# Attention and two mixture-of-experts layers on one core: the attention stage's order planned with other lengths, hops and due times

## The chip, the cores and the metric

The kernel runs on one core of one Trainium2 chip, as one program. The metric is device time in microseconds, the median of the runs shown. A core has five instruction queues that run side by side: TensorE (PE; its weight loads are listed apart as PEld), VectorE (DVE), ScalarE (ACT), GpSimd (POOL) and SyncE (SP, which here only issues DMA transfers). Each queue starts its instructions strictly in the order in which the program holds them.

## The reference

The output is a chain of three layers in float32.

- Attention over 2 batches, 8 heads, 768 tokens, head width 64. Each query and key gets a 6-bit bucket from the signs of a projection; a query sees only the keys of its own bucket: `scores = where(q_bucket == k_bucket, q·k/8, -1e9)`, softmax over keys, times `v`.
- A first mixture of 8 experts (512 to 1024 to 512) over the 1536 token rows. The router is `argmax` of the normalised row against normalised expert vectors; `out[mask] = gate * (relu(x[mask] @ w1[e]) @ w2[e])`, one expert for a token.
- A second mixture of 8 experts of the same shape with noisy logits; each token takes its best two experts and sums them by softmax weights.

## The kernel before

A float32 product is made of two or three matmuls on operands that are split into a high and a low part, so beside TensorE's work ACT makes high parts and DVE or POOL makes low parts.

**The attention stage.** The 16 (batch, head) pairs are `h`, and each has two halves of 384 queries, `g = 2h` and `g = 2h+1`, so there are 32 groups. For each group the program does, on the engines named:

- three score steps `sc` (PE, `score_pe`, line 606, four matmuls each), each into one of two PSUM buffers `S`; `mx` (DVE, line 611) takes the row maximum, `ms` (POOL, lines 616 and 617) turns it into a scale and a bias, `ex` (ACT, line 621) writes the exponentials `es` and so frees the `S` buffer;
- six transposes `tr` (PE, line 629, three matmuls each) into one of three PSUM buffers `ET`; `th` (ACT, line 633) and `tl` (DVE, line 639) split the result into `eh` and `el` and free the buffer;
- three steps `pv` (PE, lines 657 and 658, four matmuls), then `fa` (ACT), `fp` (PE, line 667, into an `ET` buffer) and `fo` (DVE, lines 681 and 683), which write the normalised rows to `xrow`.

Once per head there are also the loads of `qk` and `vr`, the split `ph` (ACT) and `pl` (POOL), the copies `hc` and `lc` (six DMAs on SP, lines 520 and 560), the bucket signs: `bp` (PE, line 579, two steps of three matmuls, each into an `ET` buffer), `bt` (DVE, line 588, two steps), and `bs`, a small DMA `ka<-qa` (SP, line 593). The first score of a head waits for that DMA.

**Other work in the same stage.** SP also writes zero rows into `xs` and `out` (line 466, 52 transfers), loads the first weights of the experts (`wraw`, line 204) and writes the rows to `xd` (line 784). ACT and POOL split four weight pieces (lines 213 and 219). When the eight groups of one half batch are done, their three row tiles are routed. Tiles `T0 = 0` can be routed after group 14, `T0 = 3` after group 15, `T0 = 6` and `T0 = 9` after groups 30 and 31. One routing is: squares of rows `rsa`, `rsb` (ACT, line 693); `r7` (DVE, line 705); `rm` (DVE, lines 699, 290, 292, 294); `rr0`, `rr` (PE, lines 243 to 253); `rq` (DVE, lines 299 and 301); `rp` (DVE, lines 266 and 269); `rn` (POOL, lines 306 to 308); `rv` (DVE, lines 311 and 312); `re` (ACT, line 315); `rg` (DVE, lines 319 to 321); three scatters `ra` (POOL, line 729, indirect DMAs of 128 rows); `rc` and `ro` (POOL). Then `e0l` (SP, line 741) loads expert 0's rows `x<-xs`; its four products with the identity and `xo` (PE, lines 745 and 780) come at the end of the stage.

**What sets the order.** Each step is given to a planner (`Plan`) with an engine, a length, a due time, the steps it depends on and the buffers it takes. The planner walks through time. On each engine it looks at the first 60 steps by due time, works out when each could start (after its dependencies, plus a hop between engines from the table `HOP`, plus a latency for DMAs), and among those that could start within `WAIT` of the first it takes the one with the least due time. What comes out is only the order of each engine's queue; on the chip each step then waits for what it needs. The two expert layers are a second `Plan` with its own steps; they begin with the matmuls of line 1062.

Of the kernel before, what the change touches and what calls it, by code (L numbers as in the profile page):

```python
# [18 lines left out]
NB, NHEAD, S, DH = 2, 8, 768, 64  # L19
# [13 lines left out]
CB = float(2.0 ** 30)  # L33
TINY = 1.1754943508222875e-38

HOP = {("PE", "ACT"): 200, ("PE", "DVE"): 200, ("ACT", "PE"): 285, ("DVE", "PE"): 280, ("POOL", "PE"): 210,
       ("ACT", "DVE"): 155, ("DVE", "ACT"): 155, ("DVE", "POOL"): 160, ("ACT", "POOL"): 120,
       ("POOL", "ACT"): 80, ("POOL", "DVE"): 90}
WAIT = 120
PR = dict(sc=-5.4, mx=-8.7, ex=-5.34, pv=3.37, fin=3.38, bits=-14.64, prep=-18.57, load=-37.69, h=-17.66, l=0)  # L40
OFF = ()
WA, WB, WS0 = 8, 5, 8
# [5 lines left out]
FSE, PVN, HLN, ESN = 0, 2, 5, 7  # L48
# [9 lines left out]
class Plan:  # L58

    def __init__(self, rings):
        self.rings = rings
        self.steps = {}

    def add(self, name, eng, dur, fn, due, deps=(), use=(), new=(), lat=0):
        self.steps[name] = (eng, dur, fn, due, tuple(deps), tuple(use) + tuple(new), tuple(new), lat)

    def order(self):
        users = {}  # L70
        for n, st in self.steps.items():
            for k in st[5]:
                users[k] = users.get(k, 0) + 1
        left, free_at, held = dict(users), {}, {r: [] for r in self.rings}
        fin, queue, clock = {}, {}, {}
        for n, st in sorted(self.steps.items(), key=lambda z: z[1][3]):
            queue.setdefault(st[0], []).append(n)
            clock[st[0]] = 0.0
        out = []
        total = sum(len(q) for q in queue.values())  # L80
        while len(out) < total:
            best = None
            for eng, q in queue.items():
                cand = []
                for n in q[:60]:
                    _, dur, _, due, deps, use, new, lat = self.steps[n]
                    t = clock[eng]
                    ok = True
                    for d in deps:
                        if d not in fin:  # L90
                            ok = False
                            break
                        t = max(t, fin[d][1] + (0 if fin[d][0] == eng else fin[d][2] + HOP.get((fin[d][0], eng), 150)))
                    if not ok:
                        continue
                    for r, k in new:
                        h = held[r]
                        if len(h) >= self.rings[r]:
                            o = (r, h[len(h) - self.rings[r]])
                            if left[o]:  # L100
                                ok = False
                                break
                            t = max(t, free_at[o] + (280 if eng == "PE" else 150))
                    if ok:
                        cand.append((t, due, n))
                if cand:
                    t0 = min(c[0] for c in cand) + WAIT
                    c = min((c for c in cand if c[0] <= t0), key=lambda z: z[1])
                    if best is None or c[0] < best[0]:
                        best = (c[0], eng, c[2])  # L110
            if best is None:
                raise RuntimeError("plan stuck: " + str({e: q[:3] for e, q in queue.items()}))
            t, eng, n = best
            _, dur, fn, due, deps, use, new, lat = self.steps[n]
            queue[eng].remove(n)
            for r, k in new:
                held[r].append(k)
            clock[eng] = t + dur
            fin[n] = (eng, t + dur, lat)
            for k in use:  # L120
                left[k] -= 1
                free_at[k] = max(free_at.get(k, 0), t + dur + lat)
            out.append((t, len(out), n))
            self.starts = out
        self.span = max(clock.values())
        return [self.steps[n][2] for _, _, n in sorted(out)]
# [7 lines left out]
def lsh_attention_moe_moe2_kernel(  # L134
# [310 lines left out]
    en = rt.tile([E, D], F32, name="en", bufs=1)  # L445
# [178 lines left out]
    EH, EL, ET, OA, OS, FO = {}, {}, {}, {}, {}, {}  # L624
# [158 lines left out]
    def r1_keep(T0):  # L783
# [1 line left out]
                          xrow[:, T0:T0 + 3, :D])  # L785


    plan = Plan(dict(S=2, ET=3, O=1, es=ESN, eh=HLN, el=HLN, ec=2, os=2, qk=3, vr=3, hx=2, lx=2, qb=2, vh=3,
                     qa=2, sm=3, rt=2))
    add = plan.add  # L790
    P = lambda f, *a, **k: (lambda: f(*a, **k))
# [5 lines left out]
    for h in range(HEADS):  # L797
        z = 12 * h
        due = lambda k, o=0.0: z + PR[k] + o
# [52 lines left out]
    for g in range(NG):  # L852
        h = g // 2
        z = 6.0 * g
        for j in range(3):
            k, o = (g, j), 2 * j
# [50 lines left out]
    for c in range(8):  # L907
        add(("wr", c), "SP", 1700, P(wload, c), (WR if c < WP else 150) + c, ([("in", 2)] if c < WP else [("in", 18 + CAP1 // 16)]) + ([("wl", c - 4, 7)] if c > 3 else []),
            lat=2500)
# [5 lines left out]
    for i, g in enumerate((14, 15, 30, 31)):  # L915
        T0, z = 3 * i, 6.0 * g + 8.5 + (L1 if i < 2 else 0)
        zg = z if i < 2 else z + 8 if i == 2 else z + 4
        hot = [("fo", x) for x in range(g % 2 + 16 * (g // 16), g + 1, 2)]
        w = L2 if i < 2 else .1
# [25 lines left out]
                [("rm", T0), ("rr0", T0)] + prev, **U)  # L945
        add(("ro", T0), "POOL", 1064, P(r1_over, T0), z + 9, [("rp", T0), ("ra", 9 if i > 1 else T0, 2)], **U)
        add(("rk", T0), "SP", 1500, P(r1_keep, T0), z + (3 if i < 3 else 0), hot)
    add(("e0l",), "SP", 2000, x0_load, 160, [("ra", 3, 2)], lat=2500)
    for d in range(4):
        x0 = [(("S", "x0"), ("ET", "x0"))[d // 2]]  # L950
        add(("e0t", d), "PE", 430, P(x0_tr, d), (180, 180, 195.1, 195.2)[d], [("e0l",), (("tr", 31, 1), ("pv", 30, 5), ("pv", 31, 5), ("pv", 31, 5))[d]] + ([("e0t", d - 1)] if d else []),
# [1 line left out]
    for i, T0 in enumerate((6, 9)):  # L953
        z = 6.0 * (30 + i) + 8.5
# [350 lines left out]
    add = plan.add  # L1305
# [24 lines left out]
    for key in range(2 * E):  # L1330
# [64 lines left out]
        t = z + 16 * q  # L1395
# [224 lines left out]
```

## Time and profile before

| | us |
|---|---|
| median of 3 runs | 784.34 |
| the runs | 784.03, 784.34, 788.62 |
| the profiled execution, its own time | 788.22 |
| its span from first to last instruction | 786.5 |

The profiled execution is near the slowest of the three runs, 3.88 above the median. In the span PE is busy 97%, PEld 94%, DVE 72%, ACT 60% and POOL 49% of the time. TensorE's granted clock is 0.995 of full speed on average. The attention stage takes the first 277.7 us: the first matmul of line 1062 starts there. A busy share over the whole span mixes the three layers; the tables by stretch and the lists in order of time are what to read. Times in such rows are in us from the start of the span; a start is exact to 0.01, the end of a matmul is modelled, so gaps are read from start to start.

### The profile page before, as it was taken

The page shows a single profiled execution, that of the slowest core. Times are in us where ns is not written, and L with a number is a line of the kernel's source. Part 1 is how long each engine was busy: PE and PEld are TensorE (multiplying, and loading weights), DVE is VectorE, ACT ScalarE, POOL GpSimd, SP SyncE. Part 2 cuts the span into 40 slices and gives each one's busy share as a digit, 9 for nine tenths or more (in the row PEclk, how much of TensorE's full clock was granted, in tenths as well). Part 3 has the DMA queues.
Part 4 walks back from the last instruction along what each step waited for, and adds up shares of the span by engine and source line. Part 5 has one row for each costly group of instructions (what it writes and reads, how often), then busy time and mean ns, then how long its engine had stood idle before and what let it go on. Part 6 is the DMA issues. An engine that isn't in the chain of part 4 may idle for free.

```text
span 786.5 us, 15056 instructions
## 1 busy us (share of the span) xinstructions
PE 759.5 (97%) x5094; PEld 735.8 (94%) x5094; DVE 565.9 (72%) x1265; ACT 473.2 (60%) x1009; POOL 384.8 (49%) x679
## 2 busy tenths in 40 slices
PE   8999999898999999999999999999999999999996
PEld 6999999787999889999999998999999999999995
DVE  8999999986989868878867767684575566565511
ACT  7899999776888747656656555454344435354310
POOL 7555654773442360443224334028374564748384
PEclk9999999999999999999999999999999999999998
DMA  7697778897662257976678656867796675866333
GB/s 188 160 281 219 173 197 239 233 243 235 148 162 58 80 163 237 274 241 192 206 237 238 214 173 187 181 182 152 168 229 146 165 175 126 178 155 108 93 34 83
DMA packets 92964, 140.64 MB, mean 179 GB/s; under 512 B 25898, under 2 KB 56898, under 8 KB 92882
## 3 DMA queue, kind: packets, MB, share of 16 engines
q1 hardware_dynamic: 75618, 122.93, 55.5%
q0 software_dynamic: 17264, 16.69, 11.7%
q8 instruction: 42, 0.69, 0.4%
q14 instruction: 40, 0.33, 0.1%
HBM read 88.54 MB, written 34.46 MB: 156 GB/s over the span
## 4 chain that ended last, share of the span: by engine, by line
PE 81%; DVE 7%; ACT 4%; DMA 3%; issue 2%; POOL 2%; POOLq 0%; another core or an unknown queue 0%; SPq 0%; ACTq 0%; DVEq 0%
PE ET L1086 9%; PE ET L1088 9%; PE S L1062 9%; PE ET L1087 9%; PE S L1064 9%; PE S L1063 9%; PE S L606 7%; PE ET L629 6%; PE O L657 3%; PE O L658 3%; PE ET L667 2%; PE ET L579 2%; DMA wraw<-in_w2a_dram 2%; PE ET L1131 1%; DVE mxs L611 1%
## 5 line engine op out<-in xcount | busy, mean ns | idle before, releaser
L1270 POOL DMA_INDIRECT out_dram<-yo,idx x91 | 148.5, 1632 | 124.6 <-DVE yo L1267 99.0
L1062 PE MATMUL S<-xh,w0h 128*128 128x224 f32 (+1 forms) x512 | 163.3, 319 | 1.4 <-DVE hl L1072 1.0
L1064 PE MATMUL S<-xh,w0l 128*128 128x224 f32 (+1 forms) x512 | 160.6, 314 | 0.0
L1063 PE MATMUL S<-xl,w0h 128*128 128x224 f32 (+1 forms) x512 | 159.5, 312 | 0.3 <-issue 0.3
L1086 PE MATMUL ET<-hh,w1h 128*128 128x224 f32 (+2 forms) x504 | 157.0, 312 | 1.9 <-ACT ys L1110 1.7
L1088 PE MATMUL ET<-hh,w1l 128*128 128x224 f32 (+2 forms) x504 | 156.9, 311 | 0.0
L1087 PE MATMUL ET<-hl,w1h 128*128 128x224 f32 (+2 forms) x504 | 155.8, 309 | 0.0
L1068 ACT ACTIVATE hh<-S 128x448 fp32r<-128x448 f32 (+1 forms) x64 | 45.1, 704 | 126.4 <-PE S L1064 118.7
L1072 DVE SCALAR_TENSOR_TENSOR hl<-S,hh 128x448 fp32r<-128x448 f32 (+1 forms) x64 | 52.4, 819 | 77.8 <-ACT hh L1068 71.7
L621 ACT ACTIVATE es<-S,mxs 128x768 f32<-128x768 f32 x96 | 95.6, 996 | 16.9 <-POOL mxs L617 12.3
L639 DVE TENSOR_TENSOR el<-ET,eh 128x384 fp32r<-128x384 f32 x192 | 99.3, 549 | 8.4 <-ACT eh L633 5.4
L611 DVE TENSOR_REDUCE mxs<-S 128x1 f32<-128x768 f32 x96 | 91.5, 954 | 15.0 <-PE S L606 12.9
L1086 PEld LDWEIGHTS ET<-hh,w1h 128*128 128x128 f32 x504 | 95.6, 190 | 3.7 <-ACT ys L1110 3.5
L1062 PEld LDWEIGHTS S<-xh,w0h 128*128 128x128 f32 x512 | 97.1, 190 | 2.0 <-DVE hl L1072 1.2
L1063 PEld LDWEIGHTS S<-xl,w0h 128*128 128x128 f32 x512 | 97.2, 190 | 1.2 <-issue 0.5
L633 ACT ACTIVATE eh<-ET 128x384 fp32r<-128x384 f32 x192 | 87.1, 492 | 18.3 <-PE ET L629 17.0
L1064 PEld LDWEIGHTS S<-xh,w0l 128*128 128x128 f32 x512 | 97.2, 190 | 0.5 <-issue 0.2
L1087 PEld LDWEIGHTS ET<-hl,w1h 128*128 128x128 f32 x504 | 95.7, 190 | 0.7
L1088 PEld LDWEIGHTS ET<-hh,w1l 128*128 128x128 f32 x504 | 95.6, 190 | 0.2
L219 DVE TENSOR_TENSOR w1l<-wraw,w1h 128x512 fp32r<-128x512 f32 x128 | 81.9, 685 | 15.5 <-ACT w1h L213 13.7
L629 PE MATMUL ET<-idf,es 128*128 128x128 f32 x576 | 85.7, 275 | 0.6 <-DVE enT L503 0.4
L213 ACT ACTIVATE w1h<-wraw 128x512 fp32r<-128x512 f32 x128 | 72.7, 623 | 14.6 <-DMA wraw<-in_w2a_dram 11.6
(260 smaller groups left out, 1443.2 us busy)
## 6 DMA issues: line engine op xcount, KB each, us to landing
wraw<-in_w1a_dram SPq DMA_DIRECT2D x32, 512.0 KB
wraw<-in_w2a_dram SPq DMA_DIRECT2D x32, 512.0 KB
wraw<-in_w1b_dram SPq DMA_DIRECT2D x32, 512.0 KB
wraw<-in_w2b_dram SPq DMA_DIRECT2D x32, 512.0 KB
xs<-zrow SPq DMA_DIRECT2D x26, 260.5 KB
xr<-xs SPq DMA_DIRECT2D x28, 208.0 KB
qk<-in_qk_dram SPq DMA_DIRECT2D x15, 384.0 KB
xs<-zrow SPq DMA_DIRECT2D x14, 261.0 KB
```

Of the source, the lines that this page charges most:

```text
L611: nc.vector.tensor_reduce(MX[(3 * g + j) % 9][:, 0:1], SC[g, j][:, :, :384], axis=AX.XY, op=OP.max, negate=True)
L621: nc.scalar.activation(ES[g, j].rearrange("p (a b) -> p a b", a=2), SC[g, j][:, :, :384], AF.Exp, bias=mx[:, 2:3], scale=mx[:, 1:2], accum ...
L629: nc.tensor.transpose(T[:, j * 128:j * 128 + 128], ES[g, j][:, kb * 128:kb * 128 + 128], idf)
L633: nc.scalar.activation(EH[g, kb], ET[g, kb], AF.Copy)
L639: nc.vector.tensor_tensor(EL[g, kb], ET[g, kb], EH[g, kb], op=OP.subtract)
L1062: nc.tensor.matmul(o, wH[n][:, fs], xh, start=kd == 0, stop=False)
L1063: nc.tensor.matmul(o, wH[n][:, fs], xl, start=False, stop=False)
L1064: nc.tensor.matmul(o, wL[n][:, fs], xh, start=False, stop=kd == 3)
L1086: nc.tensor.matmul(P, wH[n][:, ws], hh, start=f == 0, stop=False)
L1087: nc.tensor.matmul(P, wH[n][:, ws], hl_, start=False, stop=False)
L1088: nc.tensor.matmul(P, wL[n][:, ws], hh, start=False, stop=f == 7)
L1270: s = nc.gpsimd.indirect_dma_start(out=out.rearrange("n (a c) -> (n a) c", a=4), out_offset=bass.IndirectOffsetOnAxis(ap=IDX[e][:, b:b + 1 ...
```

## The change

The change touches the first planner alone, the one of the attention stage; the expert layers keep the default lengths, hops and waits.

- `LENGTH` gives new lengths to about 60 kinds of steps, and to SP's DMAs a new length and latency. `HOP` has new hops; the old table stays as `HOP0`, the default.
- `SHIFT` moves the due times of 34 kinds of steps. The kind is the step's first name, for routing steps with its `T0`, and for `ms` with its engine.
- `WAITS` replaces the one `WAIT` of 120 by a wait of each engine: none on PE, on ACT the larger of 130 and 0.4 of the candidate's length, on DVE 120, on POOL the larger of 120 and the candidate's whole length. A freed PSUM buffer counts as free for PE after 200, before 280.
- `e0l` depends on the last scatter of `T0 = 0` too, not on that of `T0 = 3` alone.

No instruction is added or removed: each of the five queues holds the same instructions as before, in another order, and the order of the expert layers is unchanged on every queue.

```diff
-HOP = {("PE", "ACT"): 200, ("PE", "DVE"): 200, ("ACT", "PE"): 285, ("DVE", "PE"): 280, ("POOL", "PE"): 210,
+HOP = {("PE", "ACT"): 260, ("PE", "DVE"): 280, ("ACT", "DVE"): 149, ("ACT", "POOL"): 195, ("DVE", "POOL"): 169,
...
+LENGTH = {('X4', 'at', 5600): 6800, ('ACT', 'ph0', 412): 407, ('DVE', 'pl0', 469): 466, ('DVE', 'pl', 469): 477, ('DVE', 'sp', 433): 806, ('ACT', 'fk0', 733): 727,
...
+SHIFT = {'bs': 5, 'bt': 15, 'en3': 10, 'fr': -60, 'fs': -40, 'fv1': 40, 'mx': -5, 'oh9': -65, 'ph': -30,
+    'pl': -5, 'pv': 5, 'ra3': 180, 'rc0': 335, 're3': 30, 'rg0': 10, 'rn6': -305, 'ro0': 155, 'rq0': 47,
+    'rq3': 55, 'rr00': 29, 'rsa0': -22.7, 'rsa3': -5, 'rsa6': 15, 'rsa9': 30, 'rsb3': -60, 'rv0': 20, 'rv3': -40,
+    'rv6': -85, 'sc': 3.5, 'th': -4, 'tl': 4, 'tr': 5.3, 'wh': -5, 'xa9': -60}
+WAITS = {'PE': (0, 0.0), 'ACT': (130, 0.4), 'DVE': (120, 0.0), 'POOL': (120, 1.0)}
 WAIT = 120
+ROUTING = ("rsa", "rsb", "r7", "rm", "rr0", "rr", "rq", "rp", "rn", "rv", "re", "rg", "ra", "rc", "ro", "xa", "xb", "oh", "xo")
...
     def add(self, name, eng, dur, fn, due, deps=(), use=(), new=(), lat=0):
+        t = self.length.get((eng, name[0], dur), dur)
+        dur, lat = t if isinstance(t, tuple) else (t, lat)
+        due += self.shift.get(self.group(name, eng), 0)
         self.steps[name] = (eng, dur, fn, due, tuple(deps), tuple(use) + tuple(new), tuple(new), lat)
...
-                            t = max(t, free_at[o] + (280 if eng == "PE" else 150))
+                            t = max(t, free_at[o] + (self.free if eng == "PE" else 150))
...
-                    t0 = min(c[0] for c in cand) + WAIT
+                    t0, _, n = min(cand, key=lambda z: z[0])
+                    w, f = self.waits.get(eng, (WAIT, 0))
+                    t0 += max(w, f * self.steps[n][1])
...
-    add(("e0l",), "SP", 2000, x0_load, 160, [("ra", 3, 2)], lat=2500)
+    add(("e0l",), "SP", 2000, x0_load, 160, [("ra", 3, 2), ("ra", 0, 2)], lat=2500)
```

In the changed kernel all lines after the tables stand 29 or 30 lines lower.

**Place 1: DVE, where the routing of `T0 = 0` begins.** `mxs` is the row maximum `mx`, `el` the low part `tl`, `lgp` and `xrow` are `fo`, `qa` is a sign step `bt`, `sm` the reciprocal `fr`; `lg`, `m`, `hot` and `z` are `rm`, `i` and `oh` are `rq`. Before, from the `fo` of group 14:

```order
L681 TENSOR_TENSOR lgp<-ET,sm 128x24
L683 TENSOR_TENSOR xrow<-ET,sm 128x3x64
L588 TENSOR_SCALAR qa_149<-ET,bthr,bval 44x384
L639 TENSOR_TENSOR el<-ET,eh 128x384
L699 TENSOR_TENSOR lg<-l_2209,lgp 128x24
L290 MAX m_2345<-lg 128x8 x3
L292 TENSOR_TENSOR hot<-lg,m_2345 128x24
L294 TENSOR_TENSOR z<-lg,m_2345 128x24
L674 RECIPROCAL sm<-sm 128x3
L299 MAX_INDEX i_2366<-m_2345,lg 128x8 x3
L301 TENSOR_TENSOR oh<-iota_87,i_2366 128x24
L611 TENSOR_REDUCE mxs<-S 128x1 x2
```

and now:

```order
L710 TENSOR_TENSOR lgp<-ET,sm 128x24
L712 TENSOR_TENSOR xrow<-ET,sm 128x3x64
L668 TENSOR_TENSOR el<-ET,eh 128x384 x2
L728 TENSOR_TENSOR lg<-l_2127,lgp 128x24
L319 MAX m_2339<-lg 128x8 x3
L321 TENSOR_TENSOR hot<-lg,m_2339 128x24
L323 TENSOR_TENSOR z<-lg,m_2339 128x24
L640 TENSOR_REDUCE mxs<-S 128x1
L703 RECIPROCAL sm<-sm 128x3
L617 TENSOR_SCALAR qa_149<-ET,bthr,bval 44x384 x2
```

`rm` stays behind the same `fo`, and `rq` no longer follows it: it stands 21 row maxima further down, just ahead of `rp`, and the whole DVE work of the two routings, which stood between the 48th and the 60th row maximum, now stands between the 46th and the 80th. The two sign steps of a head, which had low parts between them, stand behind one another, in every head from `h = 2` on but two (10 and 13).

**Place 2: POOL, the first three scatters (`xs_58`).** `mxs` are the two instructions of an `ms`, `sm` is a small sum that `fr` needs, `carry` is `rc`. Before, behind the 52nd `ms`:

```order
L671 TENSOR_SCALAR sm<-sm 128x3
L729 DMA xs_58<-xrow,pi 12288x522 x2
L616 TENSOR_SCALAR mxs<-mxs 128x1
L617 TENSOR_TENSOR mxs<-mxs 128x1
L729 DMA xs_58<-xrow,pi 12288x522
L257 TENSOR_TENSOR carry<-carry,hot 128x8
L259 TENSOR_TENSOR carry<-carry,hot 128x8 x2
```

and now, behind the 70th:

```order
L585 TENSOR_TENSOR lx<-qk,hx 128x192
L700 TENSOR_SCALAR sm<-sm 128x3
L645 TENSOR_SCALAR mxs<-mxs 128x1
L646 TENSOR_TENSOR mxs<-mxs 128x1
L758 DMA xs_58<-xrow,pi 12288x522
```

The second and third scatter follow, each behind one more `ms`; before, two scatters stood behind one another. The scatters of `T0 = 3` move from behind the 57th and 58th `ms` to behind the 77th, 83rd and 84th.

**Place 3: SP, the sign copy of head 11 (`ka_150<-qa_149`).** `wraw` are the weight loads, `xs_59` the zero rows, `qb<-lx` and `kb<-lx` the last two of the head's six copies, `qk` and `vr` a later head's loads. Before:

```order
L560 DMA qb<-lx 64x768
L560 DMA kb<-lx 64x768
L395 DMA qk<-in_qk_dram 128x768
L396 DMA vr<-in_v_dram 128x384
L204 DMA wraw<-in_w2a_dram 128x1024
L466 DMA xs_59<-zrow 16x8x521 x2
L204 DMA wraw<-in_w2a_dram 128x1024 x3
L593 DMA ka_150<-qa_149 12x768
```

and now:

```order
L589 DMA qb<-lx 64x768
L589 DMA kb<-lx 64x768
L424 DMA qk<-in_qk_dram 128x768
L425 DMA vr<-in_v_dram 128x384
L495 DMA xs_59<-zrow 16x8x521 x2
L233 DMA wraw<-in_w2a_dram 128x1024 x2
L622 DMA ka_150<-qa_149 12x768
```

The other two weight loads now stand ahead of the head's first copy. The load of expert 0's rows (line 741) moves from behind head 12's copies, ahead of head 12's sign copy, to behind head 15's copies, ahead of head 15's sign copy, the last one of the stage.

## Rows read from the trace of the kernel before

**Rows 1.** By stretch: length, busy us of PE, PEld, DVE, ACT, POOL; clock, DMA share, GB/s

```profile
30.00:130.00 100.00, 100.00 (x689) 96.51 (x687) 93.03 (x177) 91.15 (x215) 59.55 (x174) 1.00 0.76 204
130.00:190.00 60.00, 52.22 (x340) 47.80 (x337) 49.38 (x125) 45.34 (x111) 33.97 (x95) 0.97 0.90 254
190.00:255.00 65.00, 64.61 (x434) 60.98 (x433) 58.13 (x112) 55.87 (x121) 27.95 (x84) 1.00 0.52 127
255.00:277.70 22.70, 21.50 (x165) 20.40 (x164) 18.29 (x73) 16.21 (x51) 8.43 (x20) 1.00 0.21 78
```

**Rows 2.** PE in order of time: `fp` of groups 0 and 10, scores 46 and 94

```profile
28.78 0.78 PE L667 MATMUL ET<-selE,os 128*128 128x72 f32 x6
...
103.12 0.78 PE L667 MATMUL ET<-selE,os 128*128 128x72 f32 x6
...
119.86 0.51 PE L606 MATMUL S<-ka,qa 96*128 96x384 f32 x2
...
254.17 0.51 PE L606 MATMUL S<-ka,qa 96*128 96x384 f32 x2
```

**Rows 3.** What PE waited for from 125 to 200: us, times, longest

```profile
PE S L606 <- DMA ka<-qa: 3.6, 1, 3.6
PE S L606 <- ACT es L621: 2.4, 3, 1.0
PE ET L667 <- DVE el L639: 1.3, 1, 1.3
```

**Rows 4.** SP's queue and PE in order of time, and the chain of waits (last row)

```profile
169.57 2.12 SPq L204 DMA_DIRECT2D wraw<-in_w2a_dram  x3
175.34 0.81 SPq L593 DMA_DIRECT2D ka<-qa  x1
...
184.70 1.01 PE L606 MATMUL S<-ka,qa 96*128 96x384 f32 x2 [3.59 <-DMA ka<-qa]
...
175.34 9.32 DMA ka<-qa
```

**Rows 5.** The stretches in which the sign copy of head 11 is under way

```profile
160.00:185.00 25.00, 20.05 (x132) 18.06 (x131) 18.87 (x42) 17.34 (x38) 14.23 (x39) 0.99 0.99 275
185.00:190.00 5.00, 5.00 (x28) 4.71 (x27) 2.92 (x4) 2.45 (x5) 0.44 (x2) 0.73 0.89 251
```

**Rows 6.** DVE in order of time: routing steps, and a maximum with `fr` behind it

```profile
135.93 0.19 DVE L699 TENSOR_TENSOR lg<-l,lgp 128x24 f32<-128x24 f32 x1
...
137.39 0.55 DVE L639 TENSOR_TENSOR el<-ET,eh 128x384 fp32r<-128x384 f32 x1
...
142.50 0.17 DVE L311 RECIPROCAL nr<-nr 128x3 f32<-128x3 f32 x1
...
143.32 1.01 DVE L639 TENSOR_TENSOR el<-ET,eh 128x384 fp32r<-128x384 f32 x2
...
147.49 0.17 DVE L266 TENSOR_TENSOR pt<-ET,oh 128x24 f32<-128x24 f32 x1
...
148.28 0.06 DVE L299 MATCH_VALUE_LOAD i<-m,lg 128x8 f32 x1
...
152.07 0.95 DVE L611 TENSOR_REDUCE mxs<-S 128x1 f32<-128x768 f32 x1
152.94 0.17 DVE L674 RECIPROCAL sm<-sm 128x3 f32<-128x3 f32 x1
153.58 0.69 DVE L588 TENSOR_SCALAR qa<-ET,bthr,bval 44x384 fp32r<-44x384 f32 x1
```

**Rows 7.** POOL in order of time: two scatters with one `ms` between them

```profile
165.15 1.10 POOL L729 DMA_INDIRECT xs<-xrow,pi  x1 [0.46 <-DVE mxs L611]
...
167.36 1.06 POOL L729 DMA_INDIRECT xs<-xrow,pi  x1 [0.51 <-issue]
```

**Rows 8.** PE in order of time: the sign matmuls of a head and the `pv` behind them

```profile
118.56 0.40 PE L579 MATMUL ET<-hx,pst_h 128*108 128x384 f32 x1
...
119.16 0.34 PE L657 MATMUL O<-eh,vh 128*128 128x384 f32 x1
```

More of the change, by code (lines that the diff above doesn't have):

```diff
@@ L34 @@
 TINY = 1.1754943508222875e-38
-HOP = {("PE", "ACT"): 200, ("PE", "DVE"): 200, ("ACT", "PE"): 285, ("DVE", "PE"): 280, ("POOL", "PE"): 210,
+HOP = {("PE", "ACT"): 260, ("PE", "DVE"): 280, ("ACT", "DVE"): 149, ("ACT", "POOL"): 195, ("DVE", "POOL"): 169,
+       ("POOL", "ACT"): 86, ("ACT", "PE"): 165, ("DVE", "PE"): 228, ("DVE", "SP"): 110, ("POOL", "DVE"): 80,
+       ("DVE", "ACT"): 150, ("POOL", "PE"): 100, ("ACT", "SP"): 60, ("POOL", "SP"): 60, ("PE", "POOL"): 280}
+HOP0 = {("PE", "ACT"): 200, ("PE", "DVE"): 200, ("ACT", "PE"): 285, ("DVE", "PE"): 280, ("POOL", "PE"): 210,
        ("ACT", "DVE"): 155, ("DVE", "ACT"): 155, ("DVE", "POOL"): 160, ("ACT", "POOL"): 120,
        ("POOL", "ACT"): 80, ("POOL", "DVE"): 90}
+LENGTH = {('X4', 'at', 5600): 6800, ('ACT', 'ph0', 412): 407, ('DVE', 'pl0', 469): 466, ('DVE', 'pl', 469): 477, ('DVE', 'sp', 433): 806, ('ACT', 'fk0', 733): 727,
[8 rows of a table added]
+    ('SP', 'wr', 1700): (600, 7500), ('ACT', 'wh', 200): 201, ('POOL', 'wl', 417): 419, ('ACT', 'rsa', 560): 561, ('ACT', 'rsb', 240): 141, ('DVE', 'r7', 260): 237,
[4 rows of a table added]
+SHIFT = {'bs': 5, 'bt': 15, 'en3': 10, 'fr': -60, 'fs': -40, 'fv1': 40, 'mx': -5, 'oh9': -65, 'ph': -30,
[3 rows of a table added]
+WAITS = {'PE': (0, 0.0), 'ACT': (130, 0.4), 'DVE': (120, 0.0), 'POOL': (120, 1.0)}
 WAIT = 120
+ROUTING = ("rsa", "rsb", "r7", "rm", "rr0", "rr", "rq", "rp", "rn", "rv", "re", "rg", "ra", "rc", "ro", "xa", "xb", "oh", "xo")
 PR = dict(sc=-5.4, mx=-8.7, ex=-5.34, pv=3.37, fin=3.38, bits=-14.64, prep=-18.57, load=-37.69, h=-17.66, l=0)
@@ L58, with __init__ @@
 class Plan:
-    def __init__(self, rings):
-        self.rings = rings
+    def __init__(self, rings, length={}, shift={}, waits={}, group=None, hop=HOP0, free=280):
+        self.rings, self.length, self.shift, self.waits, self.hop, self.free = rings, length, shift, waits, hop, free
+        self.group = group or (lambda name, eng: name[0])
         self.steps = {}
     def add(self, name, eng, dur, fn, due, deps=(), use=(), new=(), lat=0):
+        t = self.length.get((eng, name[0], dur), dur)
+        dur, lat = t if isinstance(t, tuple) else (t, lat)
+        due += self.shift.get(self.group(name, eng), 0)
         self.steps[name] = (eng, dur, fn, due, tuple(deps), tuple(use) + tuple(new), tuple(new), lat)
@@ L92, in order @@
                             break
-                        t = max(t, fin[d][1] + (0 if fin[d][0] == eng else fin[d][2] + HOP.get((fin[d][0], eng), 150)))
+                        t = max(t, fin[d][1] + (0 if fin[d][0] == eng else fin[d][2] + self.hop.get((fin[d][0], eng), 150)))
                     if not ok:
@@ L785, in r1_keep @@
                           xrow[:, T0:T0 + 3, :D])
-    plan = Plan(dict(S=2, ET=3, O=1, es=ESN, eh=HLN, el=HLN, ec=2, os=2, qk=3, vr=3, hx=2, lx=2, qb=2, vh=3,
+    part = lambda n, eng: n[0] + eng if n[0] == "ms" else n[0] + str(n[1]) if n[0] in ROUTING else n[0]
+    plan = Plan(length=LENGTH, shift=SHIFT, waits=WAITS, group=part, hop=HOP, free=200, rings=dict(S=2, ET=3, O=1, es=ESN, eh=HLN, el=HLN, ec=2, os=2, qk=3, vr=3, hx=2, lx=2, qb=2, vh=3,
                      qa=2, sm=3, rt=2))
```

12 rows, old and new, of the table LENGTH are left out of this document.

## The prediction

> **What bounds the kernel now.** I read the table by stretch first [rows 1], because the change touches the attention stage alone. From 30 to 130 us PE is busy 100.00 of 100 us, and weight loads fill 96.51: nothing in the steady stage waits for anything but PE. From 130 to 190, where the routing of `T0 = 0` and `T0 = 3` is put between the groups, weight loads fill only 47.80 of 60 us. From 190 to 255 they fill 60.98 of 65, and at the stage's end PE is busy 21.50 of 22.70.
>
> How much was lost there comes out in two ways. By starts [rows 2]: groups 0 to 10 take 103.12 - 28.78 = 74.34 us, so 7.434 for a group; 48 scores are 16 groups, 118.9 us, but scores 46 and 94 stand 134.3 apart, 15.4 too much. By weight loads [rows 1], against the steady 96.51%: 60 - 47.80/0.965 = 10.5 and 65 - 60.98/0.965 = 1.8, and as loads also take longer where the clock was down, 1.2 more (below): 13.5. The starts also count what PE has to do there for routing, which stays. I take **14 us** as what a better order could give back at most in this middle stretch.
>
> What ended PE's waits is in the list of waits [rows 3]: 3.6 us once for the sign copy `ka<-qa`, 2.4 in three for `es` of ACT, 1.3 once for `el` of DVE. The rest is spread over many short ones.
>
> **Term A, the sign copy of head 11.** SP issues three weight loads at 169.57 and the sign copy at 175.34; it lands 9.32 us later, at 184.66, and the score behind it, first of its head, has waited 3.59 us [rows 4]. The DMA engines are 0.99 busy from 160 to 185 and move 275 GB/s [rows 5]. After the wait the granted clock is 0.73 of full speed from 185 to 190 [rows 5], a mix of its levels of 1.2 and 2.4 GHz after PE stood; 5 x (1 - 0.73) = 1.35, of which some lies under loads, so 1.2. A is 3.6 + 1.2 = 4.8.
>
> The change does three things to it. Two of the four loads move from between the zero rows and the sign copy to ahead of the head's six copies. The first three scatters leave this window (from behind the 52nd and 53rd `ms` to behind the 70th to 72nd). But the bytes that SP issues between head 10's sign copy and head 11's are the same: by the shapes in the diff and the order, four loads of 0.524 MB, four fills of 0.267, six copies of 0.197, `qk` and `vr` 0.590, in all 4.93 MB. In one undisturbed pair of groups, 14.87 us, that is 332 GB/s, above the 275 at which the engines showed 0.99. At 275 it takes 17.9 us, 3.1 too long. With three scatters (0.8 MB) it took 5.74 MB / 275 = 20.9, 6.0 too long, of which 3.6 reached PE: 2.4 were slack. By that balance 0.7 of the wait stays. Against it, the window before was itself stretched by the routing, and now is not, so the balance is kind. Bounds: nothing is recovered (0), or all (4.8). I take the middle, **2.4**, since the rate needed is nearer to the rate seen than the bytes changed.
>
> The Trainium skill says otherwise (Perfetto Trace Analysis, § Engine Utilization): a core's HBM share is 358 GB/s, and a core that is alone can reach some 120% of it. By that 332 GB/s would fit, all of A would go, and the sum would be 2.4 us better. The row, with 0.99 busy at 275 GB/s, speaks for transfers that cost the engines more than their bytes, and I go by the row.
>
> **Term B, the routing's squeeze.** 14 - 4.8 = 9.2 us. DVE is the engine that is tight: in the steady stage it is busy 93.03 of 100 us [rows 1], so 7% of the time is free for anything else. The routing of a tile group takes of DVE, in order of time [rows 6], 137.39 - 135.93 = 1.46 for `rm` and `rq`, 143.32 - 142.50 = 0.82 for `rv` and `r7`, 148.28 - 147.49 = 0.79 for `rp` and most of `rg`: about 3 us, 6 for the two. Before, this stands between the 48th and the 60th row maximum, from 135.93 [rows 6] to the scatters at 165.15 [rows 7]: 7% of 29.2 us is 2.0 of room, an overload of 4. Now it stands between the 46th and the 80th, 34 maxima or 11.3 groups, 84 us: 5.9 us of room for 6 of work. The overload falls from 4.0 to about 0.1.
>
> POOL's scatters take 1.06 to 1.10 us each with about 0.5 around them [rows 7], and a row maximum that waits for its `ms` holds one of two `S` buffers: two scatters behind one another hold a score's chain for 3 us, longer than a third of a group (2.48). That is what the `es` waits of 2.4 us [rows 3] come from, as `ex` stands behind `ms`. Now each scatter stands between two `ms`, 1.5 us behind one maximum, which two `S` buffers can cover.
>
> I leave 1.2 us for DVE (three short waits like the 1.3 of [rows 3] would be 3.9, none would be 0; the room is just used up, so nearer to none) and 0.6 for six scatters. B gives back 9.2 - 1.8 = **7.4**; bounds 0 and 9.2.
>
> **The steady cycle.** The same matmuls stand in a strictly repeating pattern of steps. PE was 100.00% busy without it, so it can gain nothing that idle time shows. It can lose: the two sign steps `bt` of a head now stand behind one another on DVE, and a third `ET` buffer is needed by the transposes behind the two sign matmuls. From the row maximum's start, DVE needs 152.94 - 152.07 = 0.87, then `fr` 0.17, then 0.69 for a `bt` [rows 6], less what overlaps, plus a way to and from PE each: about 2.1 to 2.4 us. PE's cover is the second sign step, 119.16 - 118.56 = 0.60 [rows 8], three transposes and a `pv`, 119.86 - 119.16 = 0.70 [rows 2, 8]: with the transposes about 2.1. The difference, 0 to 0.3 us in each of 15 heads, is 0 to 4; DVE's slack of 7% is 1.0 in a pair and covers most. I take **0.4** as a loss.
>
> **Other edits.** At the stage's tail, 22.70 - 21.50 = 1.2 us of PE stay [rows 1], 0 either way. `e0l` waits for two scatter sets now, and is issued behind head 15's copies: the first score of head 15 comes four scores ahead of 254.17 [rows 2], and the stage ends at 277.7 [rows 1], so the load has some 30 us. What it holds on SP is head 15's sign copy, if the last scatter, behind the 84th `ms`, is not done; that copy is needed by the 91st score, six scores or 14.9 us later, which covers a scatter. If the first cover were gone, the products with the identity would wait for a DMA of the order of [rows 4], 9.3 us. No instruction of the expert layers moves, so they start earlier by what the first stage gains.
>
> **Sum.** 2.4 + 7.4 - 0.4 = 9.4 us in the profiled execution: 788.2 - 9.4 = 778.8. That execution lies 3.9 above the median of the runs (784.34). If those 3.9 are spread over it, the changed kernel's median is 784.3 - 9.4 = 774.9; if they are the very stall of term A, the median has less to give back, and it is 778.8 - 0 = 778.8. Weighted two to one for the first: **776**.
>
> **Rivals.** A change of 1%, 7.8 us, is about what a measurement of this kernel can tell from none; that is 776.5 and 792.2.
>
> 1. *All of it comes back.* The sign copy is on time, DVE's room is enough: 14 us and the tail's 1.2, so 784.3 - 15 = 769, with some remainder up to 773. For it: the room of 5.9 against 6.0 and the fewer bytes in the window. Against: DMA at 0.99. A further gain in the steady stage would need more than idle time, since PE shows 100.00. The Trainium skill (Perfetto Trace Analysis, § Identifying the Most-Contended Engine) holds that matmul busy time is a bad measure and loads the good one: by it 3.5% of 30 to 255 us, 7.9 us, would still be open, and the regular pattern could reach some 768. No row shows what would end those gaps, so I give 768 a chance of 0.03, within this rival's.
> 2. *DVE stays the bound.* The routing steps do not fill DVE's free slots evenly, and each still delays a maximum: only A and a little of B comes back, 784.3 - 3 = 781 to 785.
> 3. *The sign copy is late again, or `e0l` is.* The DMAs issued ahead of head 11's copy are as many as before, and `e0l` now stands ahead of head 15's sign copy, the last one; B is gained and A is not, or is paid there: 784.3 - 7.4 + 1 to 5 = 778 to 782.
> 4. *Slower.* The `ET` wait behind the two sign steps opens in every head. It uses up the gain of 9.4 from 0.63 us in a head (15 heads), and from 1.15 us the kernel is 1% slower. At 1.2 us it is 18: 784.3 + 18 - 9.4 = 793, up to 796. For it: DVE's chain is by full durations as long as PE's cover. Against it: the rows allow a shortfall of 0.3 us, a quarter of that.
>
> **Chances.** Forecast, 772 to 779.5 for itself: 0.50, of which 0.30 below 776.5. Rival 1: 0.19, all faster. Rival 2: 0.12, same. Rival 3: 0.11, same. Rival 4: 0.08, slower in 0.06 and same in 0.02. Faster 0.49, same 0.45, slower 0.06. The range reaches over rivals 1 to 3, 769 to 785, and leaves out rival 4 and the edges of the others, some 0.18.
>
> **What would show it.** Right: weight loads fill over 90% from 130 to 190; no wait of `S` for the sign copy above 1.5 us; the clock at 1.00 throughout; scores 46 and 94 some 123 us apart. Term A wrong: a single wait of 3 us or more for `ka<-qa`, at head 11 or 15. Term B wrong: many waits for `el` and `es` from the 46th to the 80th maximum. The steady cycle wrong: PE below 99 of 100 us from 30 to 130, with waits of `ET` for `bt`. The start of line 1062's matmuls must move by as much as the whole does; if it does not, the cause lies where I have not looked.

## The result, and the profile after

The changed kernel takes **776.0 us** (median of 4 runs, 775.65 to 776.71); the kernel before took 785.0 in the same comparison (4 runs, 784.03 to 788.62). The ratio is 0.9874, 95% interval 0.9844 to 0.9903: 1.3% faster. The forecast was 776 in a range of 769 to 785.

The profiled executions lie differently to their medians: before's at 788.22, 3.2 above; after's at 775.65, 0.35 below. Their spans (first to last instruction) are 786.5 and 773.9, so the two traces differ by 12.6 us where the medians differ by 9.0. The parts below are parts of the 12.6.

By stretch, after, with the columns of [rows 1]:

```profile
30.00:130.00 100.00, 99.81 (x692) 97.00 (x692) 92.83 (x178) 92.59 (x217) 58.47 (x170) 1.00 0.78 208
130.00:190.00 60.00, 56.28 (x381) 53.42 (x380) 53.71 (x121) 51.61 (x128) 31.53 (x93) 1.00 0.88 236
190.00:255.00 65.00, 64.96 (x457) 63.14 (x456) 58.72 (x131) 57.54 (x130) 33.65 (x96) 1.00 0.52 135
```

Weight loads fill 53.42 of 60 us in the routing stretch, where they filled 47.80: 89%, against 96.5 in the steady stage. The clock is 1.00 where it was 0.97. PE in order of time, after, the four instructions of [rows 2], and the first matmul of the expert layers:

```profile
27.42 0.83 PE L696 MATMUL ET<-selE,os 128*128 128x72 f32 x6
...
101.40 0.79 PE L696 MATMUL ET<-selE,os 128*128 128x72 f32 x6
...
117.74 0.51 PE L635 MATMUL S<-ka,qa 96*128 96x384 f32 x2
...
242.53 0.51 PE L635 MATMUL S<-ka,qa 96*128 96x384 f32 x2
...
266.38 0.27 PE L1092 MATMUL S<-xh,w0h 128*128 128x224 f32 x1
```

The two scores stand 124.8 us apart, 134.3 before: 9.5 of the gain lie between them. The first `fp` comes 1.36 earlier than before. Ten groups take 73.98 where they took 74.34; an undisturbed pair of groups (one head) now takes 14.69 (86.71 to 101.40, from group 8 to 10) and took 14.87, and a delay of 0.4 at group 4 takes part of that back. The experts' first matmul comes at 266.38 instead of 277.71, 11.3 earlier, and the rest of the span is 507.5 against 508.8.

Of the signs that the prediction named, the sign copy's wait is gone, the clock is 1.00 in all three stretches, and the two scores stand 1.8 further apart than the 123 named; weight loads fill 89% of the routing stretch, just short of 90.

What PE waited for from 125 to 200 us, after (as [rows 3]):

```profile
PE S L635 <- ACT es L650: 1.9, 1, 1.9
PE ET L658 <- DVE el L668: 1.7, 1, 1.7
```

The sign copy `ka<-qa` is gone from the list. Both waits that are left stand close together, at 169 and 175 us, and have one origin. SP in order of time:

```profile
153.39 2.15 SPq L233 DMA_DIRECT2D wraw<-in_w2a_dram  x2
...
160.44 0.59 SPq L424 DMA_DIRECT2D qk<-in_qk_dram  x1
163.77 0.35 SPq L425 DMA_DIRECT2D vr<-in_v_dram  x1
...
168.64 0.81 SPq L622 DMA_DIRECT2D ka<-qa  x1
```

A row of what SP itself waited for from 120 to 180 us:

```profile
SPq L425 <- DMA wraw<-in_w2a_dram: 2.3, 1, 2.3
```

ACT, POOL and PE in order of time:

```profile
167.40 0.84 ACT L541 ACTIVATE hx<-qk 128x768 fp32r<-128x768 f32 x1 [3.11 <-PE ET L658]
169.60 1.72 POOL L585 TENSOR_TENSOR lx<-qk,hx 128x192 fp32r<-128x192 f32 x3 [3.75 <-DMA qk<-in_qk_dram]
...
169.27 0.55 PE L658 MATMUL ET<-idf,es 128*128 128x128 f32 x3 [1.68 <-DVE el L668]
175.13 0.59 PE L635 MATMUL S<-ka,qa 96*128 96x384 f32 x2 [1.92 <-ACT es L650]
```

Two weight loads, issued at 153.39 ahead of head 11's six copies, keep the DMA engines busy; SP waits 2.3 us for one of them between `qk` and `vr`. ACT then stands 3.11 us at the split of head 13, whose `hx` buffer is the one that head 11's copies read, and POOL 3.75 at its low part. Behind that split stand `th` and `ex`, so PE stops for 1.7 and 1.9. The releasers in the brackets of the split's two rows are not to be taken at their word: the transposes and the `qk` load that they name fit no dependence of head 13 that was still open. What the split waited for stands in the trace's semaphore events. The last copy from head 11's `hx`, issued at 157.50, landed at 167.22, and the split started at 167.40; the last copy from its `lx`, issued at 159.54, landed at 169.35, and POOL's part started at 169.60. These copies took 8.5 to 9.9 us from issue to landing. That the weight loads are the cause is shown below, by the runs that move them.

### The profile page after: what moved, and what is told of

It reads as the page before. It is cut to its first block, busy times and chain, and to the rows that moved or that the text cites. A ratio compares the mean times of both kernels' runs of the same rounds, so it can differ in the third digit from the quotient of the medians.

```text
span 773.9 us, 15040 instructions
## 1 busy us (share of the span) xinstructions
PE 752.7 (97%) x5094; PEld 735.3 (95%) x5094; DVE 562.0 (73%) x1265; ACT 473.2 (61%) x1009; POOL 393.3 (51%) x679
## 5 line engine op out<-in xcount | busy, mean ns | idle before, releaser
L1300 POOL DMA_INDIRECT out_dram<-yo,idx x91 | 155.1, 1704 | 118.0 <-DVE yo L1297 92.4
L668 DVE TENSOR_TENSOR el<-ET,eh 128x384 fp32r<-128x384 f32 x192 | 101.3, 551 | 10.2 <-ACT eh L662 8.9
L662 ACT ACTIVATE eh<-ET 128x384 fp32r<-128x384 f32 x192 | 89.1, 490 | 13.0 <-PE ET L658 10.1
L658 PE MATMUL ET<-idf,es 128*128 128x128 f32 x576 | 88.8, 274 | 2.1 <-DVE el L668 1.7
L248 DVE TENSOR_TENSOR w0l<-wraw,w0h 128x512 fp32r<-128x512 f32 x120 | 75.7, 687 | 8.1 <-ACT w0h L242 8.0
```

The costliest lines, as they stand in the source:

```text
L248: eng.tensor_tensor(wL[n][:, c], wraw[n][:, c], wH[n][:, c], op=OP.subtract)
L662: nc.scalar.activation(EH[g, kb], ET[g, kb], AF.Copy)
L668: nc.vector.tensor_tensor(EL[g, kb], ET[g, kb], EH[g, kb], op=OP.subtract)
L1300: s = nc.gpsimd.indirect_dma_start(out=out.rearrange("n (a c) -> (n a) c", a=4), out_offset=bass.IndirectOffsetOnAxis(ap=IDX[e][:, b:b + 1 ...
```

## The experiments

Each kernel keeps the changed kernel's code and its instructions and moves steps between two orders. `plan_a` holds the steps with the new tables, `plan_b` with the old ones; `merged(host, donor, moved)` takes each engine's queue from the host and puts each moved step behind the step behind which it stands in the donor. With nothing moved it gives the order of after, or of before.

```diff
+def merged(host, donor, moved):
...
+    for i, (_, _, n) in enumerate(sorted(donor.starts)):
+        e = steps[n][0]
+        q = queue[e]
+        if moved(n):
+            j = pos[e] = max(pos.get(e, 0), q.index(last[e]) + 1)
+            q.insert(j, n)
...
+        else:
+            last[e] = n
```

"Ratio" is to the kernel before in the same comparison, a value under 1 being faster; "stage end" is the start of the experts' first matmul in the profiled execution.

| run | order | us | ratio, 95% interval | stage end |
|---|---|---|---|---|
| before | old | 785.0 | 1 | 277.7 |
| after | new | 776.0 | 0.9874 (0.9844 to 0.9903) | 266.4 |
| e1 | old, again | 788.6 | one run | 276.9 |
| e2 | old, routing steps at new places | 786.1 | 1.0008 (0.9990 to 1.0026) | 276.2 |
| e9 | the same, placed by maxima | 785.1 | 1.0035 (1.0015 to 1.0054) | 275.8 |
| e3 | new, routing steps at old places | 790.6 | 1.0066 (1.0040 to 1.0092) | 278.9 |
| e7 | old, scatters at new places | 780.8 | 0.9962 (0.9938 to 0.9985) | 271.4 |
| e5 | old, four weight loads late | 781.7 | 0.9963 (0.9942 to 0.9984) | 272.3 |
| e10 | new, loads back, routing packed as before but scatters away | 781.0 | 0.9974 (0.9956 to 0.9993) | 271.2 |
| e8 | new, sign steps at old places | 794.3 | 1.0136 (1.0109 to 1.0163) | 285.1 |
| e4 | new, all early weight loads back | 771.7 | 0.9827 (0.9803 to 0.9850) | 262.6 |
| e12 | new, last four loads back | 771.8 | 0.9854 (0.9824 to 0.9884) | 263.3 |
| e6 | new, last four in groups 23 and 24 | 773.5 | 0.9868 (0.9842 to 0.9894) | 264.6 |
| e11 | new, last four behind the last sign copy | 770.7 | 0.9843 (0.9814 to 0.9872) | 261.8 |

Before's own median went from 782.7 to 785.8 between the comparisons, so a difference of 3 us between two medians of different rows is not to be relied on. Stage ends have a catch too. Before's 277.7 comes from an execution 3.2 above its median, and in every row with a ratio the stage end shows 1.4 to 4.7 us more of a gain on it than the ratio does (e9: 1.9 us earlier, and slower by the ratio). A gain over before is therefore to be read from the ratio; stage ends are of use between the other rows.

**e1, the kernel before once more.** No edit.

> The kernel before, unchanged, for a second profile of it. If the 3.9 us by which the profiled execution lay above the median are the late sign copy of head 11 (wait of 3.6 us), this profile shows a shorter wait there and a span some 3 us shorter, and the expert layers take 508.8 us as before; if they are spread, the wait is again 3 us or more.

The sign copy's wait was 2.7 us, the stage ended at 276.9, and the execution still took 788.57, the experts 510.0. One execution, again above the median, cannot exclude the stall as part of the excess; but e5 below has no such stall, and its profiled execution still lies 2.25 above its median. So the stall alone does not make the excess, and where it lies stays open.

**e2 and e9, routing alone.**

```diff
-    for f in plan.order():
+    for f in merged(plan_b, plan_a, lambda n: (n[0] in ROUTING[:15] + ("rk",) and n[1] < 6) or n[0] == "e0l"):
```

and for e9 the anchor restricted:

```diff
-            last[e] = n
+            last[e] = n if e == "SP" or n[0] in ("mx", "ms", "ex", "sc") else last.get(e)
```

> Order of before, in which only the routing steps of T0 = 0 and 3 (and e0l) stand at the places of the changed kernel, behind the same steps. Theory of the prediction (routing's squeeze is most of the gain, 7.4 of 9.4): 777 to 778.5. Rival, the regular steady pattern gives 0.17 us for each pair of groups, 2.6 in all, and routing the rest: 778.5 to 780. Rival, weight loads on SP are what matters: 782 or more.

> As the run with routing alone moved, but each moved step stands behind the same row maximum (DVE), ms (POOL), exponential (ACT) or score (PE) as in the changed kernel, instead of the same next-door step. If that run's null came of the exact neighbours, this gains: 777 to 781. If the old order has no room for routing spread out, whatever its neighbours: 784 to 788.

Neither gained; e9 is slower by its interval. The theory of the prediction fails here as stated: spreading the routing is worth nothing by itself. The loss has moved. In e2 weight loads fill 50.83 us from 130 to 190, 3.0 more than before, but 59.01 from 190 to 255, 2.0 less, and PE's waits from 125 to 200 us are several, the longest of 1.5 us, none for the sign copy. How a routing step costs something there, ACT, DVE and PE of e9 in order of time:

```profile
120.18 0.82 PE L658 MATMUL ET<-idf,es 128*128 128x128 f32 x6
120.36 0.57 ACT L722 ACTIVATE sqj<-xrow 128x448 f32<-128x448 f32 x1
120.83 0.19 ACT L722 ACTIVATION_READ_ACCUMULATOR sqj<-xrow 128x1 f32 x1
121.05 0.58 ACT L722 ACTIVATE sqj<-xrow 128x448 f32<-128x448 f32 x1
...
121.83 0.85 ACT L662 ACTIVATE eh<-ET 128x384 fp32r<-128x384 f32 x2
...
122.33 1.02 DVE L668 TENSOR_TENSOR el<-ET,eh 128x384 fp32r<-128x384 f32 x2 [0.64 <-ACT eh L662]
...
122.94 0.55 PE L658 MATMUL ET<-idf,es 128*128 128x128 f32 x3 [0.72 <-DVE el L668]
```

Two squares of rows behind one another push `eh` back, `el` behind it, and the transposes behind that: 0.72 us of PE for 1.3 of ACT. In the changed kernel the same two squares stand just as close:

```profile
118.45 0.33 PE L608 MATMUL ET<-hx,pst_h 128*108 128x384 f32 x1
118.65 0.58 ACT L722 ACTIVATE sqj<-xrow 128x448 f32<-128x448 f32 x1
119.35 0.58 ACT L722 ACTIVATE sqj<-xrow 128x448 f32<-128x448 f32 x1
119.50 0.49 PE L658 MATMUL ET<-idf,es 128*128 128x128 f32 x3
120.03 0.49 ACT L662 ACTIVATE eh<-ET 128x384 fp32r<-128x384 f32 x1
```

There PE is in the six sign matmuls meanwhile, the next transposes start only at 119.50, and no wait for `eh` or `el` follows. In e9 six transposes start at 120.18, ahead of the squares, and their `eh` has to wait for ACT.

**e3, everything but routing.** As e2 with host and donor exchanged.

> Order of the changed kernel, in which only the routing steps of T0 = 0 and 3 (and e0l) stand behind the steps they stood behind before. Theory of the prediction: only the sign copy's part comes back, less 0.4 of steady loss: 783 (782 to 785). Rival, steady pattern: 2.6 plus part of the sign copy's wait: 779 to 782. Rival, weight loads: 776 to 779.

Slower than every branch. The new order takes up `fr` early on DVE and `fs` early on POOL; with the routing packed at its old place `fr` waits for `fs` and PE for `el` (one wait of 3.4 us near 150, the clock 0.84 from 130 to 160), and PE waits 4.8 more in three for `es`. At group 18 it is 14.0 us behind the changed kernel; after that point its pairs are no longer than that kernel's.

**e7, the scatters alone.**

```diff
+    for f in merged(plan_b, plan_a, lambda n: (n[0] in ("ra", "ro") and n[1] < 6) or n[0] == "e0l"):
```

> Order of before; only the six scatters of T0 = 0 and 3 with the overflow step behind them (and e0l) stand at the places of the changed kernel, DVE's routing steps stay. If the scatters between the maxima and the DMA traffic they bring are what the squeeze consisted of: 780 to 782. If it is DVE's work, or nothing moves without the new steady order: 784.5 to 787.

The first branch, 780.8, a gain of 3.0 us by the ratio (1.2 to 4.9). What PE waited for from 125 to 200 us:

```profile
PE ET L696 <- DVE el L668: 1.3, 1, 1.3
PE S L635 <- DMA ka<-qa: 1.0, 1, 1.0
PE ET L272 <- POOL carry L288: 0.4, 1, 0.4
```

Against [rows 3] the three waits for `es` are gone and the sign copy's is 1.0 instead of 3.6. The wait of DVE's `el` stays, as DVE's steps did. Since e2 moves these scatters too and gains nothing, the other routing steps at their new places must lose in the old order about what the scatters gain.

**e5, the four loads out of the window, in the old order.** A third plan gives those loads one more dependence, and the host takes their places from it.

```diff
+    add = lambda n, e, d, f, z, p=(), **k: (plan_a.add(n, e, d, f, z, p, **k), plan_b.add(n, e, d, f, z, p, **k), plan_c.add(n, e, d, f, z, list(p) + [("ex", 23, 0)] * (n[0] == "wr" and n[1] > 3), **k))
...
+    for f in merged(plan_b, plan_c, lambda n: n[0] == "wr"):
```

> Order of before; only the last four early weight loads (around head 11's sign copy) stand later on SP, in groups 23 to 24. It measures the prediction's term A where it arose. If the sign copy's wait is worth its 3.6 us and the clock behind it: 785.8 - 4.8 = 781 (780 to 783), no wait for ka<-qa, clock 1.00. Rival, another wait takes its place, since DVE and POOL are behind with the routing anyway: 785 to 786.

What PE waited for from 125 to 200 us:

```profile
PE S L635 <- ACT es L650: 2.4, 3, 1.0
PE ET L696 <- DVE el L668: 1.3, 1, 1.3
PE ET L272 <- POOL carry L288: 0.4, 1, 0.4
```

Term A, measured where it arose: the stage ends 5.4 us earlier than in before's profile and 4.6 earlier than in e1's, and by the ratio the kernel gains 2.9 us of 785 (1.3 to 4.6). The prediction's 4.8 was the right size for the profiled executions and too much for the median. No other wait took its place.

**e10, routing packed in the new order.**

```diff
+    for f in merged(plan_a, plan_b, lambda n: (n[0] in ROUTING[:12] + ("rc", "rk") and n[1] < 6) or n[0] == "wr"):
```

> Order of the changed kernel with the weight loads back (771.7), and of the routing only the scatters at the changed places: the DVE, ACT, PE and POOL steps ahead of them stand packed behind the steps they stood behind before. Theory of the prediction (spreading DVE's 6 us of routing over 84 us is worth some 4): 775 to 777, losses between the 46th and 60th maximum. Rival, the new steady order takes routing anywhere once the scatters are away: 771 to 773. Rival, packed steps collide with the new order: above 778.

The third branch: 781.0. It differs from e4 only by the places of the routing steps ahead of the scatters and of `rc`, and ends the stage 8.6 us later. That arises between groups 14 and 16, which take 24.15 us from `fp` to `fp` against 15.41 in e4. DVE and PE there, in order of time:

```profile
145.37 0.17 DVE L295 TENSOR_TENSOR pt<-ET,oh 128x24 f32<-128x24 f32 x1
...
146.71 0.18 DVE L330 TENSOR_TENSOR oh<-iota,i 128x24 f32<-128x24 f32 x1
148.87 0.18 DVE L703 RECIPROCAL sm<-sm 128x3 f32<-128x3 f32 x1 [1.98 <-POOL sm L700]
148.96 0.53 DVE L668 TENSOR_TENSOR el<-ET,eh 128x384 fp32r<-128x384 f32 x1
...
149.55 0.90 PE L658 MATMUL ET<-idf,es 128*128 128x128 f32 x3 [3.40 <-DVE el L668]
```

Routing fills DVE without a break from 145.37 to 146.89 (ten more instructions stand between the first two rows); then `fr` waits 1.98 for `fs`, which POOL reaches late, because its own routing step (1.4 us from 145.58) had waited for ACT's squares. This one knot costs PE 3.4 us in one wait, and behind it the granted clock is 0.70 from 150 to 160. That is term B's mechanism, but with three engines in it and not DVE's share alone, and in one place.

**e8, sign steps apart.**

```diff
+    for f in merged(plan_a, plan_b, lambda n: n[0] in ("bp", "bt") and n[1] > 1):
```

> Order of the changed kernel; only the sign steps (bp on PE, bt on DVE, from head 2 on) stand where they stood before, the two of a head apart. The undisturbed pairs of groups took 14.87 before and 14.69 now, and two sign steps side by side take 1.05 where two apart take 2 x 0.60: if that is the gain of the steady cycle, it is lost again, 0.15 x 14 = 2.1: 778 to 779, pairs of 14.84. If the rest of the pattern makes it, 776 and 14.69. If the sign steps at old places wait for DVE in the new order: 780 or more.

The third branch: 794.3. The steady stretch by the table of [rows 1]:

```profile
30.00:130.00 100.00, 98.00 (x649) 90.56 (x648) 86.75 (x166) 87.99 (x203) 54.40 (x158) 1.00 0.72 193
```

and what PE waited for in it:

```profile
PE ET L658 <- DVE qa L617: 1.2, 7, 0.2
PE ET L658 <- DVE el L668: 0.3, 1, 0.3
```

A pair takes 15.6 to 15.9 us instead of 14.7; the 0.93 between 15.62 and 14.69, in 15 heads, is 14 of the 18.7 us by which the stage ends later. The rest comes behind 130 us, with a wait of 3.8 for `el` and the clock at 0.91 from 170 to 190. The list of waits holds 1.5 us in the steady stretch and PE is busy 98 of 100, but weight loads fell from 97.00 to 90.56. By the starts, the step behind `fp`, one double transposes step and one score of a pair take 0.23, 0.45 and 0.15 us longer than such steps elsewhere: this is a loss that only the loads and the starts show in full.

**e4, e12, e6, e11, the weight loads in the new order.** e4 moves `n[0] == "wr"` back, e12 only those with `n[1] > 3`; e6 and e11 take the places of `plan_c`, the latter with `("bs", 15, 0)` in place of `("ex", 23, 0)`.

```diff
+    for f in merged(plan_a, plan_b, lambda n: n[0] == "wr" and n[1] > 3):
```

> Order of the changed kernel, with the eight early weight loads alone behind the steps they stood behind before (four of them together ahead of head 11's sign copy). Theory of the prediction: the 2.4 us of the sign copy are lost again: 778 to 779, with a wait for ka<-qa. Rival, the loads' place is worth nothing once the scatters are away: 776 within 0.7.

> Order of the changed kernel; only the four weight loads around head 11's copies stand behind the steps they stood behind before (one behind the qk and vr loads, three behind the zero rows), the first early loads stay where the change put them. If the two loads ahead of head 11's copies are what the changed kernel lost (SP waits for a load on the way to vr, the split of head 13 waits 3.1 us): 771.5 to 773, no wait of the score for es above 1 us, stage end near 263. If the first early loads carry the 4.3 us: 776.

> Order of the changed kernel, with the first early weight loads where they stood before and the last four in groups 23 to 24. If the loads' place in the changed kernel only costs because head 13's qk load stands behind two of them (4.3 us by the run with the loads back), this is as that run: 771 to 772.5. If DMA crowding in that stretch costs anything beyond that, 769.5 to 771.

> Order of the changed kernel, the first early weight loads where they stood before, the last four behind the last sign copy of the stage (head 15). No sign copy and no qk load can be late behind them: 769.5 to 771.5, no wait for ka<-qa. Rival: the expert layers miss the loads at their start and the gain is given back there: 772 to 775.

Undoing the loads' move makes the kernel faster, the reverse of the prediction. e4 missed both of its branches, and e12 met the first of its two. With the four loads back (one behind `vr`, three behind the zero rows, all ahead of head 11's sign copy), PE's list of e12 from 125 to 200 us holds one row:

```profile
PE S L635 <- issue: 0.4, 1, 0.4
```

and the split of head 13, in ACT's order of time, comes 2 us earlier:

```profile
165.42 0.85 ACT L541 ACTIVATE hx<-qk 128x768 fp32r<-128x768 f32 x1 [0.77 <-PE ET L608]
```

Head 11's copies took 3.6 to 4.3 us from issue to landing there, and the last landed at 162.58, well before the split. So the pair ahead of head 11's copies cost the changed kernel 3.1 us at the stage's end, 4.2 by the medians, 1.6 by the ratios' centres (intervals overlap). My expectation for e6 put it on head 13's `qk` load, but that had been issued at 143.4 and landed at 148.3; the landings show head 11's copies. e6 gained less than expected: near group 24 its loads delay a sign copy again (one wait of 1.5 us, at 203.97). e11 has no such wait, ends the stage at 261.8 and is the fastest seen, 770.7; between it and e4 the runs cannot tell.

## Why the prediction was right, and where its steps were not

**The number and the sign.** 776 forecast, 776.0 measured. That they agree this closely is luck: the gain between the traces was 12.6 where 9.4 was summed, and the excess of before's profiled execution hid the difference. The weighting of the two readings of that execution is not borne out by anything: the stall of term A alone does not make the 3.9 us (e1, e5), and the rest of the excess is not explained.

**Term A, the sign copy.** Sized rightly for the profiled execution (4.8; e5 shows 5.4 at the stage's end, 2.9 by the ratio), and it is gone, as rival 1 had it. But I booked 2.4 us of it to two loads that move earlier and to the scatters. The scatters did it: they alone cut the wait from 3.6 to 1.0 (e7), and with the loads at their old place in the new order it does not appear at all (e4, e12). The moved loads made a new loss of 3 to 4 us at the stage's end (e12, e4), at the copies of the same head. The step that failed is the one that looked only at who waits at the end of SP's window, and not at what stands behind the two loads at their new place: six copies whose landing frees two buffers, and which took 8.5 to 9.9 us there instead of 3.6 to 4.3 (e12).

**The weighing of the rate.** I held that 4.93 MB in a pair of groups would not fit at the 275 GB/s of a stretch in which the engines showed 0.99. In e12 the same bytes are issued between the two sign copies, from 151.68 to 167.04, and head 11's is on time. Ten us of that stretch, in the changed kernel and in e12:

```profile
160.00:170.00 10.00, 8.32 (x57) 7.95 (x56) 7.90 (x17) 6.75 (x16) 2.47 (x10) 1.00 1.03 209
160.00:170.00 10.00, 10.00 (x71) 9.82 (x70) 9.87 (x22) 8.94 (x20) 5.40 (x16) 1.00 1.03 321
```

At the same full share the engines moved 209 GB/s in the one and 321 in the other, so the 275 was no ceiling; and part of the bytes went out behind the pair, as the mean from 151.68 to 167.04 is 242. By the Trainium skill (Perfetto Trace Analysis, § Engine Utilization), which gives 358 GB/s as a core's share of HBM, the 332 would have fit and all of A would go. That outcome is what came, though a whole pair did not reach the rate.

**Term B, the routing.** 7.4 forecast. In the new order, spreading the steps ahead of the scatters is worth 8.6 at the stage's end (e10 to e4). In the old order spreading all of it is worth nothing (e2, e9). The argument by DVE's room gave a fair size by a rule that does not hold in general: the same room existed in the old order. My reading is that what decides is whether each step falls where the engine's next step has slack, and that this goes with the order it was planned in; the two squares of e9 are one place that shows it, and no run isolates it. The POOL part, scatters behind one another, was right: the `es` waits are gone with the scatters alone (e7).

**The steady cycle.** Wrong sign: 0.4 lost was forecast, a pair got 0.18 shorter, some 2.7 us over 15 pairs. The two sign steps of a head side by side take 1.05 us, and two apart took 0.60 each [rows 8]. PE after, in order of time:

```profile
103.76 0.33 PE L608 MATMUL ET<-hx,pst_h 128*108 128x384 f32 x1
...
104.81 0.49 PE L658 MATMUL ET<-idf,es 128*128 128x128 f32 x3
105.06 0.42 PE L686 MATMUL O<-eh,vh 128*128 128x384 f32 x1
...
105.83 0.49 PE L658 MATMUL ET<-idf,es 128*128 128x128 f32 x3
```

It is not the standing together that counts, but what stands ahead. A `pv` behind transposes takes 0.77 to 0.79 us from start to start (105.06 to 105.83), behind a sign step or a score 0.70 [rows 2, 8], and a score likewise. Before, nine scores, `pv` and sign steps of a pair stand behind transposes or `fp`, and now eight, as the sign steps follow a score; that is 0.09 of the 0.18, and the rest stays open. PE's 100.00 busy hid that; weight loads, 96.51 before and 97.46 in e4, show it. The feared wait for the `ET` buffer came in none of the new order's undisturbed pairs. But apart, in the new order, the steps cost 0.93 a pair (e8), most of it in short waits: rival 4's price, from the opposite arrangement.

**The ends.** The stage's start gave 1.4 us and the experts 1.3, which I had at nothing; groups 28 to the end took 0.6 more. Two profiles of the kernel before differ by 1.2 in the experts (508.8, and 510.0 in e1), so that part may be no effect of the change. No wait of PE names `e0l`, as forecast.

So the 12.6 between the traces are 1.4 at the start, 0.5 to group 12, 10.0 from group 12 to 28, less 0.6 at the tail, and 1.3 in the experts. Groups 0 to the stage's end make 9.9 of them, where 9.4 was forecast, and that too is luck: the loads' loss of some 3 and the steady gain of some 2.7, both unforeseen, about cancel. The start and the experts made 2.7 of the excess of 3.2. That the medians nevertheless differ by 9.0 only is the unexplained excess of before's profiled execution.

## What to carry to other kernels

The parts of a planned order are not additive: here the routing's places alone gained nothing, all the rest alone was 0.7% slower, and together they gave 1.3% (1.7% with the loads back), so a sum of parts read from the old trace is an estimate of a joint effect only. A large load that is moved out of one window must be costed where it lands: list what is issued behind it and which buffers those transfers free. And an engine that is 100% busy can still have a per cent or more in how its steps are grouped; compare starts over a period, not busy time.

## What the runs showed of the hardware

- Four matmuls of a `pv` or a score take 0.70 us from start to start behind another such step and 0.77 to 0.80 behind transposes, with nothing waiting (before and after, 72 to 103 us): what stands next to what on PE costs time that no wait shows.
- SP itself waits for earlier transfers: 2.3 us for a 512 KB weight load before it could issue `vr`, which uses another buffer. The trace's semaphores show why: the program's transfers on SP count up eight semaphores in turn, and in this stage each waits until the eighth before it has landed. The second of the two weight loads, issued at 154.20, is the eighth before `vr`; it landed at 163.36, and `vr` was issued at 163.77.
- A busy share of the DMA engines says little of their rate: at 1.03 they moved 209 GB/s in the changed kernel and 321 in e12, over the same ten us.
- A longer stop of PE was followed by a lower clock: behind the 3.4 us of e10, 0.70 was granted from 150 to 160, a mix of its levels of 1.2 and 2.4 GHz, and behind the 3.6 of the kernel before, 0.73 from 185 to 190 [rows 5]. The changed kernel's stops of 1.7 and 1.9 left it at 1.00.
